# Interleaving each LayerNorm with the residual loop in front of it, in a four-layer attention and gMLP kernel

## The chip, the cores and the metric

The kernel runs on one core of a Trainium2 chip. The metric is the device time of one execution in microseconds (us). The kernel before takes 2619.56 us, the median of 5 runs (2618.32 to 2621.13). In what follows ScalarE is shown as ACT, VectorE as DVE, TensorE's matmuls as PE and its weight loads as PEld.

## The reference

A stream `x` of 2048 rows by 512 columns passes through four layers. Layers 1 and 3 are multi-query attention (A), layers 2 and 4 are gMLP (B). Each has a LayerNorm in front and a residual add behind. Both A layers share their weights, and so do both B layers.

```python
x = A_x
x = x + _A_ref(_layernorm(x), wq, wk, wv, wo)        # 32 heads of 16, one k and one v
x = x + _B_ref(_layernorm(x), w_in, w_sp, b_sp, w_out)
x = x + _A_ref(_layernorm(x), wq, wk, wv, wo)
x = x + _B_ref(_layernorm(x), w_in, w_sp, b_sp, w_out)
```

`_layernorm` subtracts the row mean and divides by `sqrt(var + 1e-5)`. It has no weights of its own.

## The kernel before

X stays in SBUF as 16 tiles of 128 rows by 512 columns, so every LayerNorm works on 16 tiles. A small scheduler takes instructions in program order: each engine has its own in-order list, and waits between engines are semaphores. **The order in which the Python code adds instructions is therefore the order in which each engine runs them.** No compiler moves them later.

The residual loop of a layer makes a tile's output on TensorE, adds it to X on VectorE, and then takes the next LayerNorm's statistics of that tile, also on VectorE:

```python
def ln_stats_tile(tt, waits):                  # VectorE
    # bn_stats (X tile -> 6 numbers a row), bn_aggr (-> mean, var), then
    # lnve = var + LN_EPS
    ...

def emit_woproj(tt, bank):                     # residual loop of attention
    # 8 matmuls of 128x512 into one PSUM bank
    ...
    er = sch.add("dve", lambda v, tt=tt, bank=bank: v.tensor_tensor(
        X[:, tt, :], PS[:, bank, 0:D], X[:, tt, :], op=ALU.add), [last])
    ...
    if not is_last_layer:
        next_stats[tt] = ln_stats_tile(tt, [er])
...
for tt in range(NT):
    emit_woproj(tt, tt % 6)                    # gMLP's loop is alike, with 7 matmuls
```

When all 16 tiles are through, the next layer begins with a LayerNorm phase of its own. The phase normalises each tile on ScalarE, transposes it on TensorE with four matmuls against an identity matrix, and copies the transposed tile out of PSUM. The copies alternate between VectorE and ScalarE:

```python
def layernorm_phase(ev_stats):
    for tt in range(NT):
        ... # ScalarE: Sqrt.  VectorE: reciprocal, and nmr = -mean * reciprocal
    ...
    def finish_copy(item):
        ...
        if tt % 2 == 0:
            e_cp = sch.add("dve", lambda v, src=src, dst=dst: v.tensor_copy(dst, src), [last_pe])
        else:
            e_cp = sch.add("act", lambda s, src=src, dst=dst: s.activation(dst, src, ACT.Copy), [last_pe])
        ...
    for tt in range(NT):
        bufi = tt % 2                          # two xn buffers
        e_xn = sch.add("act", ... xn2[:, bufi, :], X[:, tt, :], ACT.Identity,
                       bias=nmr, scale=reciprocal ...)
        bank = tt % 8
        for kc in range(KC):                   # KC = 4 transposes
            last_pe = sch.add("pe", ... PS[:, bank, ...], xn2[:, bufi, ...], ident ...)
        pend.append((tt, bank, last_pe))
        if len(pend) > 1:
            finish_copy(pend.pop(0))
    ...
```

The softmax here doesn't subtract the row's maximum and nothing guards it: scores larger than these inputs give would overflow.

## Time and profile before

The program is a row of stages that follow one another. I read their borders from the trace: the first kT matmul, the load of the Exp table, the first residual add, the first matmul of the gMLP layer, and so on. A few matmul records can be missing from a trace, so such a border may be off by a few tenths of a us. "Boundary" is the stretch from the first residual add of one layer to the first matmul of the next.

| stage of before | us | how often |
|---|---|---|
| start: loads, statistics, first LayerNorm | 37.3 | 1 |
| q, k, v projections | 24.9, 25.3 | 2 |
| attention core (Exp stage) | 936.5, 936.8 | 2 |
| boundary attention to gMLP | 44.1 | 2 |
| GELU of w_in | 93.6 | 2 |
| rest of gMLP up to its first residual add | 156.1 | 2 |
| boundary gMLP to attention | 44.1 | 1 |
| last residual loop and output | 26.7 | 1 |

The page's chain of waits, followed back from the last instruction, gives shares of the span by engine and then by line:

```profile
ACT 68%; PE 19%; DVE 11%; issue 1%; DMA 0%; SPq 0%; ACTq 0%
ACT regA L473 62%; PE PS L689 8%; PE PS L488 4%; PE PS L457 3%; DVE regB L599 2%; ACT g_sg L597 2%; PE PS L391 2%; DVE lnst L313 2%; ACT g_zb L580 1%; ACT xn L346 1%; PE PS L708 1%; DVE zst L626 1%; DVE regB L659 1%; DVE X L524 1%; DVE regA L497 1%
```

The Exp on ScalarE (line 473 of before) holds 62% of the span in this chain. It lies outside the change (ScalarE is busy 922.68 of 936.48 us in row 2 below), so the question is what the four stretches with a LayerNorm cost. Line numbers are those of the kernel that the lines come from. The table of stretches (columns: stretch in us, its length, busy us and instruction count of each engine, granted TensorE clock, DMA share, GB/s) shows the start, one Exp stage, and the two parts of one attention-to-gMLP boundary:

```profile
core 0: us, PE busy (x) PEld busy (x) DVE busy (x) ACT busy (x) POOL busy (x), PEclk, DMA share, GB/s
4.84:37.33 32.49, 9.52 (x64) 5.57 (x65) 24.03 (x88) 18.75 (x39) 5.29 (x6) 1.00 0.62 162
62.21:998.69 936.48, 803.04 (x4138) 154.41 (x4138) 148.53 (x97) 922.68 (x690) 0.00 (x0) 0.67 0.02 5
998.69:1026.50 27.81, 17.49 (x80) 7.01 (x80) 26.15 (x66) 3.04 (x15) 0.00 (x0) 0.89 0.99 197
1026.50:1042.81 16.31, 9.52 (x64) 5.56 (x65) 8.96 (x40) 15.71 (x24) 0.00 (x0) 0.50 0.96 180
```

Rows 3 and 4 are the point. In the residual part VectorE is busy 26.15 of 27.81 us while ScalarE works 3.04. In the LayerNorm part it is the other way round: ScalarE 15.71 of 16.31, VectorE 8.96. So the two halves of a boundary have different limiting engines and follow one another. The timeline of before shows one tile of the residual part (columns: start, duration, engine, line, operation, operands, count, and in brackets the idle time before and who ended it):

```profile
1000.42 0.68 DVE L524 TENSOR_TENSOR X<-PS,X 128x512 bf16<-128x512 f32 x1
...
1001.14 0.69 DVE L313 BATCH_NORM_STATS2 lnst<-X 128x6 f32<-128x512 bf16 x1
...
1001.87 0.18 DVE L315 BATCH_NORM_AGGREGATE lnmv<-lnst 128x2 f32<-128x6 f32 x1
1002.08 0.15 DVE L316 TENSOR_SCALAR lnve<-lnmv 128x1 f32<-128x1 f32 x1
1002.15 0.68 DVE L524 TENSOR_TENSOR X<-PS,X 128x512 bf16<-128x512 f32 x1
1002.27 0.20 ACT L323 ACTIVATE lnve<-lnve 128x1 f32<-128x1 f32 x1 [1.53 <-DVE lnve L316]
```

From add to add is 1002.15 - 1000.42 = 1.73 us, all of it VectorE. ScalarE waits 1.53 us of each period for its one square root. The timeline of the LayerNorm part of before:

```profile
1033.06 0.60 ACT L340 ACTIVATE xnT<-PS 128x512 bf16<-128x512 f32 x1
...
1033.56 1.50 ACT L346 ACTIVATE xn<-X,lnr 128x512 bf16<-128x512 bf16 x2
1033.76 0.69 DVE L338 CAST xnT<-PS 128x512 bf16<-128x512 f32 x1 [1.22 <-PE PS L353]
...
1034.41 1.10 PE L353 MATMUL PS<-ident,xn 128*128 128x128 bf16 x6 [0.69 <-ACT xn L346]
1035.06 0.60 ACT L340 ACTIVATE xnT<-PS 128x512 bf16<-128x512 f32 x1
```

Two tiles take 2.00 us on ScalarE (1033.06 to 1035.06: one copy and two normalisations, back to back), so a tile costs 1.00 us, and PE and VectorE both wait for ScalarE. Two groups of instructions of before, the copies on ScalarE and its square roots, will be compared with those of after (columns: line, engine, operation, operands, count, then busy us, mean ns of one, and idle us of the engine just before them):

```profile
L340 ACT ACTIVATE xnT<-PS 128x512 bf16<-128x512 f32 x32 | 19.0, 594 | 2.8 <-PE PS L353 2.8
L323 ACT ACTIVATE lnve<-lnve 128x1 f32<-128x1 f32 x64 | 13.0, 203 | 202.1 <-DVE lnve L316 202.1
```

ScalarE stood idle for 202.1 us in front of its 64 square roots. Of these, 117.3 us are the three waits for the first tile of a boundary (13.78, 89.78 and 13.77 us), which end before the residual loop is under way; 68.9 us are the 45 waits of 1.53 us inside the three residual loops; the rest is in the start.

### The profile page before, as it was taken

How to read it: one execution, taken by the hardware profiler on the slowest of the kernel's cores; microseconds unless marked ns; L12 is line 12 of the kernel's file. 1: busy time of each engine (PE TensorE's matmuls, PEld its weight loads, DVE VectorE, ACT ScalarE, POOL GpSimd, SP SyncE). 2: the span in 40 equal slices, each digit the busy share in tenths (PEclk: the TensorE clock that was granted, in tenths of full speed). 3: DMA queues.
4: the chain of work that ended last, by engine and by line, in shares of the span. 5: the costliest groups of instructions: out<-in, count | busy, mean ns of one | idle time of the engine just before them, and what ended most of it. 6: DMA issues, size and time to landing. Idle time of an engine off the chain costs nothing.

```text
span 2619.3 us, 25140 instructions
## 1 busy us (share of the span) xinstructions
PE 2153.3 (82%) x10680; PEld 526.5 (20%) x10680; DVE 716.5 (27%) x1246; ACT 2084.6 (80%) x1814; POOL 128.8 (5%) x139
## 2 busy tenths in 40 slices
PE   5888888888888887659978888888888888875599
PEld 2111111111111113113431111111111111131143
DVE  5011111112111116673341111111211111177732
ACT  4999999999999993442059999999999999933410
POOL 1000000000000000331000000000000000003300
PEclk9666766667666667679976676666766666676799
DMA  3000000000000006000000000000000000060000
GB/s 93 5 5 5 5 5 5 5 8 5 5 5 5 5 5 133 1 0 1 1 1 5 5 5 5 5 5 9 5 5 5 5 5 5 8 130 1 0 1 33
DMA packets 85488, 34.93 MB, mean 13 GB/s; under 512 B 75680, under 2 KB 80800, under 8 KB 85376
## 3 DMA queue, kind: packets, MB, share of 16 engines
q1 hardware_dynamic: 84832, 30.58, 5.5%
q0 software_dynamic: 544, 2.76, 0.3%
q8 instruction: 83, 1.36, 0.2%
q14 instruction: 29, 0.24, 0.0%
HBM read 6.05 MB, written 2.10 MB: 3 GB/s over the span
## 4 chain that ended last, share of the span: by engine, by line
ACT 68%; PE 19%; DVE 11%; issue 1%; DMA 0%; SPq 0%; ACTq 0%
ACT regA L473 62%; PE PS L689 8%; PE PS L488 4%; PE PS L457 3%; DVE regB L599 2%; ACT g_sg L597 2%; PE PS L391 2%; DVE lnst L313 2%; ACT g_zb L580 1%; ACT xn L346 1%; PE PS L708 1%; DVE zst L626 1%; DVE regB L659 1%; DVE X L524 1%; DVE regA L497 1%
## 5 line engine op out<-in xcount | busy, mean ns | idle before, releaser
L473 ACT ACTIVATE regA<-PS 128x1536 bf16<-128x1536 f32 (+1 forms) x1376 | 1840.4, 1611 | 3.8
L488 PE MATMUL PS<-regA 128*32 128x512 bf16 x4096 | 989.8, 534 | 7.8 <-DVE regA L497 7.1
L457 PE MATMUL PS<-regA 32*128 32x512 bf16 x4096 | 732.8, 526 | 260.3 <-ACT regA L473 243.3
L497 DVE COPY regA<-PS 128x512 f32<-128x512 f32 x64 | 41.2, 686 | 1459.9 <-PE PS L488 1459.9
L457 PEld LDWEIGHTS PS<-regA 32*128 32x128 bf16 x4096 | 140.5, 96 | 1025.5 <-ACT regA L473 1002.8
L488 PEld LDWEIGHTS PS<-regA 128*32 128x32 bf16 x4096 | 158.4, 100 | 525.1 <-issue 487.0
L510 DVE RECIPROCAL regA<-regA 128x512 f32<-128x512 f32 x64 | 214.3, 3349 | 115.7 <-DMA regA<-regA 115.7
L583 POOL TENSOR_TENSOR g_t<-g_zb 128x512 bf16<-128x512 bf16 x120 | 118.5, 990 | 2275.4 <-ACT g_zb L580 2275.1
L689 PE MATMUL PS<-regA,regB 128*128 128x512 bf16 x896 | 203.1, 380 | 1.7 <-ACT g_zb L580 1.7
L323 ACT ACTIVATE lnve<-lnve 128x1 f32<-128x1 f32 x64 | 13.0, 203 | 202.1 <-DVE lnve L316 202.1
L671 PE MATMUL PS<-xnT,w_in 128*128 128x512 bf16 x224 | 80.7, 505 | 73.0 <-ACT g_zb L580 72.9
L580 ACT ACTIVATE g_zb<-PS 128x512 bf16<-128x512 f32 x120 | 67.5, 568 | 91.3 <-DVE regB L599 80.9
L597 ACT ACTIVATE g_sg<-g_t 128x512 bf16<-128x512 bf16 x120 | 72.1, 601 | 81.4 <-DVE g_t L595 81.0
L639 PE MATMUL PS<-w_in,xnT 128*128 128x512 bf16 (+1 forms) x256 | 78.8, 464 | 44.8 <-ACT g_zb L580 44.5
L689 PEld LDWEIGHTS PS<-regA,regB 128*128 128x128 bf16 x896 | 83.1, 98 | 107.5 <-issue 14.5
L599 DVE TENSOR_TENSOR regB<-g_zb,g_sg 128x512 bf16<-128x512 bf16 x120 | 77.8, 649 | 85.8 <-ACT g_sg L597 85.8
L353 PE MATMUL PS<-ident,xn 128*128 128x128 bf16 x256 | 38.9, 307 | 72.6 <-ACT xn L346 48.4
L695 DVE TENSOR_TENSOR regB<-PS,regB 128x512 bf16<-128x512 f32 x56 | 37.8, 689 | 138.3 <-PE PS L692 138.3
L521 PE MATMUL PS<-wop,regB 128*128 128x512 bf16 x256 | 59.9, 398 | 1.8 <-DVE X L524 1.8
L595 DVE TENSOR_TENSOR g_t<-g_t,g_zb 128x512 bf16<-128x512 bf16 x120 | 49.9, 416 | 4.1
L346 ACT ACTIVATE xn<-X,lnr 128x512 bf16<-128x512 bf16 x64 | 48.7, 804 | 0.5
L708 PE MATMUL PS<-w_out,regB 128*128 128x512 bf16 x224 | 48.7, 379 | 0.0
(56 smaller groups left out, 599.7 us busy)
## 6 DMA issues: line engine op xcount, KB each, us to landing
regA<-regA SPq DMA_DIRECT2D x256, 32.0 KB, 1.9
X<-in_A_x_dram SPq DMA_DIRECT2D x4, 512.0 KB, 5.5
out_dram<-X SPq DMA_DIRECT2D x4, 512.0 KB, 2.9
w_in<-in_B_w_in_dram POOLq DMA_DIRECT2D x1, 1792.0 KB, 9.4
w_out<-in_B_w_out_dram POOLq DMA_DIRECT2D x1, 896.0 KB, 11.5
wq<-in_A_wq_dram SPq DMA_DIRECT2D x1, 512.0 KB, 8.2
wop<-in_A_wo_dram SPq DMA_DIRECT2D x4, 128.0 KB, 4.4
regA<-in_B_w_sp_dram SPq DMA_TRANSPOSE x32, 5.1
```

The costliest lines, as they stand in the source:

```text
L346: e_xn = sch.add("act", lambda s, tt=tt, bufi=bufi: s.activation(xn2[:, bufi, :], X[:, tt, :], ACT.Identity, bias=lnr[:, 1, tt:tt + 1], sc ...
L457: last = sch.add("pe", lambda tt_, g=g, e=e, bank=bank, t=t, b=b, cq=cq: tt_.matmul(PS[:, bank, 0:QW], kT[32 * g:32 * g + 32, e, t * 128:( ...
L473: ev_act[u] = sch.add("act", lambda s, q=q, slot=slot, n=n: s.activation(Ering[:, slot, 0:n * QW], PS[:, 3 * q:3 * q + n, :].rearrange("p ...
L488: last = sch.add("pe", lambda tt_, j=j, i=i, t=t, pp=pp, slot=slot: tt_.matmul(PS[32 * j:32 * j + 32, 6 + pp, 0:QW], vaug[:, t, :], Ering[ ...
L510: v2 = sch.add("dve", lambda v, pp=pp: v.reciprocal(rden[pp], denb[pp]), [pt])
L580: a1 = sch.add("act", lambda s, bi=bi, w=w, zap=zap: s.activation(g_zb[:, bi, 0:w], zap, ACT.Copy), [pe_last] + gbuf_free[bi])
L583: p1 = sch.add("pool", lambda g, bi=bi, w=w: g.tensor_tensor(g_t[:, bi, 0:w], g_zb[:, bi, 0:w], g_zb[:, bi, 0:w], op=ALU.mult), [a1])
L597: a2 = sch.add("act", lambda s, bi=bi, w=w: s.activation(g_sg[:, bi, 0:w], g_t[:, bi, 0:w], ACT.Sigmoid, scale=GELU_SIG_SCALE), [v3])
L599: v4 = sch.add("dve", lambda v, bi=bi, w=w, dst_ap=dst_ap: v.tensor_tensor(dst_ap, g_zb[:, bi, 0:w], g_sg[:, bi, 0:w], op=ALU.mult), [a2])
L639: last = sch.add("pe", lambda t, tt=tt, kc=kc, f0=f0, w=w, bank=bank: t.matmul(PS[:, bank, 0:w], xnT[:, kc, tt * 128:(tt + 1) * 128], w_in ...
L671: last = sch.add("pe", lambda t, fc=fc, kc=kc, t0=t0, tw=tw, bank=bank: t.matmul(PS[:, bank, 0:tw], w_in[:, kc, fc * 128:(fc + 1) * 128], ...
L689: last = sch.add("pe", lambda t, fc=fc, sc=sc, t0=t0, tw=tw, bank=bank: t.matmul(PS[:, bank, 0:tw], z2n[:, sc, fc * 128:(fc + 1) * 128], w ...
```

## The change

The intent is to run the LayerNorm of a tile as soon as that tile's residual add is done, inside the residual loop, rather than in a phase behind it. The start does the same directly behind its statistics.

```diff
-        def layernorm_phase(ev_stats):
-            ... (all 16 square roots, then 16 tiles of normalise, transpose, copy)
+        class LNPipe:
+            def tile(self, tt, stats_ev, x_ready):
+                e_sq = ... ACT.Sqrt ...
+                self.pend_sc.append((tt, e_sq, x_ready))
+                if len(self.pend_sc) > 1:             # scaling lags one tile
+                    self._scale(*self.pend_sc.pop(0))
+            def _scale(self, tt, e_sq, x_ready):
+                ... reciprocal and nmr on VectorE, normalise on ScalarE into xn2[tt % 6]
+                self.pend_pe.append((tt, bufi, e_xn))
+                if len(self.pend_pe) > 3:             # transposes lag four tiles
+                    self._trans(*self.pend_pe.pop(0))
+            def _trans(self, tt, bufi, e_xn):
+                bank = 5 + tt % 3                     # three PSUM banks
+                ... four transposes
+                self.pend.append((tt, bank, last_pe, holder))
+                if len(self.pend) > 1:                # copies lag five tiles
+                    self._finish(self.pend.pop(0))
+            def _finish(self, item):
-                if tt % 2 == 0:
+                if False:
                     ... copy on VectorE
                 else:
                     ... copy on ScalarE
+            def flush(self): ... empties the three queues
 
-                if not is_last_layer:
-                    next_stats[tt] = ln_stats_tile(tt, [er])
+                if next_ln is not None:
+                    st = ln_stats_tile(tt, [er])
+                    next_ln.tile(tt, st, er)
 
-                emit_woproj(tt, tt % 6)
+                emit_woproj(tt, tt % 5)
+            if next_ln is not None:
+                next_ln.flush()
```

Three smaller things come with it. There are six xn buffers (they lie on the end of a region that is free at that time) in place of two. The residual matmuls use banks 0 to 4, so that 5 to 7 are left for the transposes. All 64 PSUM copies run on ScalarE, where 32 ran on VectorE before.

More of the change, by code (lines that the diff above doesn't have):

```diff
@@ L62, in _flatten_waits @@
             wl.extend(_flatten_waits(w))
+        elif isinstance(w, dict):
+            assert "ev" in w, "unresolved pipeline placeholder"
+            wl.extend(_flatten_waits([w["ev"]]))
         else:
@@ L228, in build @@
         zve = sb("zve", [128, NT], FP32)
-        xn2 = sb("xn2", [128, 2, D], BF16)
         xnT = sb("xnT", [128, KC, S], BF16)
@@ L240, in build @@
         regB = sb("regB", [128, regB_elems], BF16)
+        xn2 = regB[:, regB_elems - 6 * D:regB_elems].rearrange("p (b d) -> p b d", b=6)
         z1T = regB[:, 0:NFC * S].rearrange("p (a b) -> p a b", a=NFC)
@@ L318, in ln_stats_tile, with __init__ @@
             return e3
-        def layernorm_phase(ev_stats):
-            e_nmr_t = {}
-            for tt in range(NT):
-                e_sq = sch.add("act", lambda s, tt=tt: s.activation(
-                    lnve[:, tt:tt + 1], lnve[:, tt:tt + 1], ACT.Sqrt), [ev_stats[tt]])
+        class LNPipe:
+            def __init__(self):
+                self.ev_xnT = {}
+                self.pend = []
+                self.xn_free = [None] * 6
+                self.pend_pe = []
+                self.pend_sc = []
+            def tile(self, tt, stats_ev, x_ready):
+                e_sq = sch.add("act", lambda s, tt=tt: s.activation(
+                    lnve[:, tt:tt + 1], lnve[:, tt:tt + 1], ACT.Sqrt), [stats_ev])
+                self.pend_sc.append((tt, e_sq, x_ready))
+                if len(self.pend_sc) > 1:
+                    self._scale(*self.pend_sc.pop(0))
+            def _scale(self, tt, e_sq, x_ready):
                 e_r = sch.add("dve", lambda v, tt=tt: v.reciprocal(lnr[:, 0, tt:tt + 1], lnve[:, tt:tt + 1]), [e_sq])
-                e_nmr_t[tt] = sch.add("dve", lambda v, tt=tt: v.scalar_tensor_tensor(
+                e_nmr = sch.add("dve", lambda v, tt=tt: v.scalar_tensor_tensor(
                     out=lnr[:, 1, tt:tt + 1], in0=lnmv[:, tt, 0:1], scalar=-1.0, in1=lnr[:, 0, tt:tt + 1],
                     op0=ALU.mult, op1=ALU.mult), [e_r])
-            ev_xnT = {}
-            xn_free = [None, None]
-            pend = []
-            def finish_copy(item):
-                tt, bank, last_pe = item
-                src = PS[:, bank, 0:KC * 128].rearrange("p (kc c) -> p kc c", kc=KC)
-                dst = xnT[:, :, tt * 128:(tt + 1) * 128]
-                if tt % 2 == 0:
-                    e_cp = sch.add("dve", lambda v, src=src, dst=dst: v.tensor_copy(dst, src), [last_pe])
-                else:
-                    e_cp = sch.add("act", lambda s, src=src, dst=dst: s.activation(dst, src, ACT.Copy), [last_pe])
-                bank_free[bank] = [e_cp]
-                ev_xnT[tt] = e_cp
-            for tt in range(NT):
-                bufi = tt % 2
+                bufi = tt % 6
                 e_xn = sch.add("act", lambda s, tt=tt, bufi=bufi: s.activation(
@@ L348, in layernorm_phase @@
                     bias=lnr[:, 1, tt:tt + 1], scale=lnr[:, 0, tt:tt + 1]),
-                    [e_nmr_t[tt], xn_free[bufi], X_tile_ready[tt]])
-                bank = tt % 8
+                    [e_nmr, self.xn_free[bufi], x_ready])
+                self.pend_pe.append((tt, bufi, e_xn))
[3 more added lines that the diff above has]
+                bank = 5 + tt % 3
                 last_pe = None
@@ L356, in layernorm_phase, with flush, events @@
                         ([e_xn, ev_ident] + bank_free[bank]) if kc == 0 else [])
-                bank_free[bank] = ["pending"]
-                xn_free[bufi] = last_pe
-                pend.append((tt, bank, last_pe))
-                if len(pend) > 1:
-                    finish_copy(pend.pop(0))
-            while pend:
-                finish_copy(pend.pop(0))
-            return [ev_xnT[tt] for tt in range(NT)]
+                holder = {}
+                bank_free[bank] = [holder]
+                self.xn_free[bufi] = last_pe
+                self.pend.append((tt, bank, last_pe, holder))
+                if len(self.pend) > 1:
+                    self._finish(self.pend.pop(0))
+            def _finish(self, item):
+                tt, bank, last_pe, holder = item
+                src = PS[:, bank, 0:KC * 128].rearrange("p (kc c) -> p kc c", kc=KC)
+                dst = xnT[:, :, tt * 128:(tt + 1) * 128]
+                if False:
+                    e_cp = sch.add("dve", lambda v, src=src, dst=dst: v.tensor_copy(dst, src), [last_pe])
+                else:
+                    e_cp = sch.add("act", lambda s, src=src, dst=dst: s.activation(dst, src, ACT.Copy), [last_pe])
+                holder["ev"] = e_cp
+                bank_free[bank] = [e_cp]
+                self.ev_xnT[tt] = e_cp
+            def flush(self):
+                while self.pend_sc:
+                    self._scale(*self.pend_sc.pop(0))
+                while self.pend_pe:
+                    self._trans(*self.pend_pe.pop(0))
+                while self.pend:
+                    self._finish(self.pend.pop(0))
+            def events(self):
+                assert len(self.ev_xnT) == NT, "LN pipeline incomplete"
+                return [self.ev_xnT[tt] for tt in range(NT)]
         evac_ctr = [0]
@@ L373, in evac_copy, with attention_layer @@
             return sch.add("dve", lambda v, src=src, dst=dst: v.tensor_copy(dst, src), waits)
-        def attention_layer(ev_stats, is_last_layer):
-            all_xnT = layernorm_phase(ev_stats)
+        def attention_layer(all_xnT, next_ln):
             ev_kT = []
@@ L563, in attention_layer, with gmlp_layer @@
             for tt in range(NT):
-                emit_woproj(tt, tt % 6)
-        def gmlp_layer(g_wsp, ev_stats, is_last_layer):
+                emit_woproj(tt, tt % 5)
+            if next_ln is not None:
+                next_ln.flush()
+        def gmlp_layer(g_wsp, all_xnT, next_ln):
             for sc in range(NKT):
@@ L569, in gmlp_layer @@
                         waits=list(shared_state["regA_free"]))
-            all_xnT = layernorm_phase(ev_stats)
             gbuf_free = [[] for _ in range(GNB)]
@@ L702, in gmlp_layer @@
             for tt in range(NT):
-                bank = gi % 8
+                bank = tt % 5
                 tci = (tt * 128) // 512
@@ L714, in gmlp_layer @@
                 X_tile_ready[tt] = er
-                if not is_last_layer:
-                    next_stats[tt] = ln_stats_tile(tt, [er])
+                if next_ln is not None:
+                    st = ln_stats_tile(tt, [er])
+                    next_ln.tile(tt, st, er)
                 gi += 1
-        next_stats = [ln_stats_tile(tt, [x_part_group[tt]]) for tt in range(NT)]
+            if next_ln is not None:
+                next_ln.flush()
         X_tile_ready = [x_part_group[tt] for tt in range(NT)]
+        shared_state = {"regA_free": []}
+        ln0 = LNPipe()
+        for tt in range(NT):
+            st = ln_stats_tile(tt, [x_part_group[tt]])
+            ln0.tile(tt, st, x_part_group[tt])
+        ln0.flush()
+        cur_ln = ln0
         bi_ = 0
-        shared_state = {"regA_free": []}
         for li, Lt in enumerate(layer_types):
-            cur_stats = list(next_stats)
             is_last = (li == len(layer_types) - 1)
-            if cfg.get("barrier", False):
-                sch.barrier()
+            next_ln = None if is_last else LNPipe()
+            all_xnT = cur_ln.events()
             if Lt == "A":
-                attention_layer(cur_stats, is_last)
+                attention_layer(all_xnT, next_ln)
             else:
-                gmlp_layer(g_wsp_list[bi_], cur_stats, is_last)
+                gmlp_layer(g_wsp_list[bi_], all_xnT, next_ln)
                 bi_ += 1
+            cur_ln = next_ln
         nparts = 4 if NT % 4 == 0 else 1
```

## The prediction

> **What bounds it now.** The chain of waits is 62% the Exp on ScalarE in the two attention stages (from the stretches view: 62 to 986 us and 1361.5 to 2286 us, ScalarE busy 922 of 924 us in each). The change doesn't touch them. The u product (109 us twice, TensorE busy 108.7) and the GELU stages (about 139 us twice, a ScalarE/VectorE/Pool loop) aren't touched either. What it touches are the four LayerNorm stretches. In the timeline of before:
> - Start: statistics from 4.8 us at 1.0 us a tile, then 16 square roots done, then normalise/transpose/copy from 21.3 to 37.3 us. This phase is ScalarE-bound: two xn (0.75 us apart) and one copy (0.5 us) make 2.0 us per two tiles; ScalarE is busy 15.7 of 16.5 us.
> - Attention to gMLP (twice): VectorE runs residual add 0.72, statistics 0.73, aggregate and epsilon 0.29, 1.73 us a tile, from 998.7 to 1026.4 us; only then the LayerNorm phase, 16.3 us, to 1042.8. ScalarE is busy 3 of the first 27.8 us.
> - gMLP to attention: the same from 1292.5 to 1320.3, then 16.3 us, to 1336.7.
>
> **What the change does.** The LayerNorm of a tile follows its residual add in a pipeline, transposes 4 tiles behind on TensorE, so most of the 16.3 us phase hides under the residual phase. All 16 PSUM copies move to ScalarE (VectorE loses 32 casts of 0.69 us). No work is removed. I considered table switches, since Sqrt now alternates with Identity and Copy. The Trainium skill ("ScalarE: Activation LUTs", Table sets) says that copy and identity are in every set; before's trace agrees (one load of 1.28 us at the first Sqrt, none between Sqrt and xn and copy), and the built program still has 12 loads. So no cost.
>
> **Costs of the merged phase, per tile.** VectorE: 1.73 plus reciprocal and nmr 0.27 = 2.0 us. TensorE: after attention 8 matmuls at 0.216 = 1.73 plus four transposes about 0.33 = 2.06; after gMLP 7 at 0.216 = 1.51 plus 0.33 = 1.84. ScalarE: sqrt 0.15-0.2, xn 0.75, copy 0.5 = about 1.45. So after attention VectorE and TensorE are nearly tied, about 2.06 us; after gMLP VectorE, 2.0; at the start (no residual add; VectorE 1.28) ScalarE, about 1.45.
>
> The merged phase thus lengthens by 0.27-0.33 us x 16 = 4.3-5.2 us, and a tail stays after the last residual add: statistics, sqrt, xn, then five ScalarE copies, two of which gate the last transposes: about 5.7 us from the last add to the last transpose (before: 18.1).
>
> Gains, all on the critical path (estimates from the above): start, last transpose at about 30.6 instead of 37.3: 6.7; attention to gMLP 7.5 each, twice; gMLP to attention 8.4. Sum 30 us. TensorE may also be warmer at the next stage (before: granted clock 0.50 in the LayerNorm phase, first 8 matmuls 0.43 us each): 0 to 2 us a boundary, mostly lost since the tail is sparse too.
>
> **Prediction: 2589 us**, 1.2% less; 80% range 2578 to 2600. Faster by over 2%: 0.03; within 2%: 0.95; slower: 0.02.
>
> **Right if:** first kT matmuls start near 30.6 us; the residual phases take about 32-33 us rather than 27.8; the LayerNorm-only part falls from 16.3 to about 4-5 us; Exp stages keep 924 us.
>
> **Wrong if:** the merged loop settles above 2.2 us a tile (waits between the four engines, or a half clock on TensorE after its wait for the first transpose), which costs 3 us per boundary for each 0.2; ScalarE at the start takes more than 1.6 us a tile; or GELU stages shift their rhythm by a few us.

## The result, and the profile after

The kernel after takes 2583.82 us, the median of 7 runs (2581.33 to 2584.86). Before takes 2619.45 us in 13 runs (2618.32 to 2621.13). The ratio is 0.9864 (95% interval 0.9854 to 0.9874), which is within 2%. A ratio here is the mean time of one kernel's fast runs over that of the other's of the same rounds, so it is not quite the ratio of the quoted medians. The result is correct.

The gain of the medians is 35.6 us. The prediction had 30.

| stage | before | after | gain |
|---|---|---|---|
| start, to first kT matmul | 37.33 | 28.54 | 8.79 |
| boundary attention to gMLP, 1st | 44.12 | 35.27 | 8.85 |
| boundary gMLP to attention | 44.14 | 35.28 | 8.86 |
| boundary attention to gMLP, 2nd | 44.13 | 35.27 | 8.86 |
| **these four together** | | | **35.4** |
| Exp stages, both | 1873.25 | 1873.85 | -0.6 |
| projections and GELU, two of each | 237.4 | 231.9 | 5.6 |
| rest of gMLP before the residual add, both | 312.2 | 312.7 | -0.5 |

The four places give 35.4 us, which is the gain of the medians within the spread. The spans of the two profiled executions differ by more, 2619.3 - 2579.5 = 39.8 us. This pair is an extreme one: the profiled run of before was its slowest (2621.13), that of after its fastest (2581.33). The excess sits in the projections and the GELU stages. I come back to it below, because "TensorE is warmer there" would be a tempting reading.

The same views of after. The chain of waits by engine:

```profile
ACT 69%; PE 18%; DVE 11%; issue 1%; DMA 0%; SPq 0%; ACTq 0%
ACT regA L497 64%; PE PS L715 8%; PE PS L512 4%; PE PS L481 3%; DVE regB L625 3%; ACT g_sg L623 2%; PE PS L415 2%; ACT g_zb L606 1%; DVE lnst L316 1%; PE PS L734 1%; DVE zst L652 1%; DVE regB L685 1%; DVE X L548 1%; DVE regA L521 1%; PE PS L718 1%
```

The shares barely changed (Exp is now line 497), and the chain alone would not have told where 36 us came from. The table of stretches does (the first boundary is cut where the last VectorE instruction of the loop is done):

```profile
core 0: us, PE busy (x) PEld busy (x) DVE busy (x) ACT busy (x) POOL busy (x), PEclk, DMA share, GB/s
4.84:28.54 23.70, 9.40 (x65) 5.57 (x65) 18.88 (x80) 20.66 (x47) 5.29 (x6) 1.00 0.84 222
52.47:989.06 936.59, 799.49 (x4130) 153.40 (x4130) 148.52 (x96) 922.80 (x690) 0.00 (x0) 0.67 0.02 5
989.06:1021.70 32.64, 25.27 (x140) 12.07 (x140) 29.96 (x97) 20.24 (x42) 0.00 (x0) 0.84 1.02 194
1021.70:1024.33 2.63, 1.28 (x12) 0.98 (x13) 0.00 (x0) 2.63 (x7) 0.00 (x0) 0.83 1.08 178
```

The residual part grew from 27.81 to 32.64 us and now holds 20.24 us of ScalarE work that used to stand behind it. What is left of the LayerNorm part is 2.63 us, from 16.31. The timeline of after, one tile of the merged loop:

```profile
1004.78 0.68 DVE L548 TENSOR_TENSOR X<-PS,X 128x512 bf16<-128x512 f32 x1
1004.90 0.81 ACT L344 ACTIVATE regB<-X,lnr 128x512 bf16<-128x512 bf16 x1
1005.50 0.70 DVE L316 BATCH_NORM_STATS2 lnst<-X 128x6 f32<-128x512 bf16 x1
1005.62 0.58 ACT L374 ACTIVATE xnT<-PS 128x512 bf16<-128x512 f32 x1
1006.23 0.18 DVE L318 BATCH_NORM_AGGREGATE lnmv<-lnst 128x2 f32<-128x6 f32 x1
...
1006.35 0.39 PE L356 MATMUL PS<-ident,regB 128*128 128x128 bf16 x4
1006.45 0.15 DVE L319 TENSOR_SCALAR lnve<-lnmv 128x1 f32<-128x1 f32 x1
...
1006.52 0.15 DVE L339 RECIPROCAL lnr<-lnve 128x1 f32<-128x1 f32 x1
...
1006.64 0.20 ACT L332 ACTIVATE lnve<-lnve 128x1 f32<-128x1 f32 x1 [0.44 <-DVE lnve L319]
1006.71 0.16 DVE L340 SCALAR_TENSOR_TENSOR lnr<-lnmv,lnr 128x1 f32<-128x1 f32 x1
```

VectorE again has no gap that ends in a wait: add 0.72, statistics 0.73, aggregate 0.22, epsilon 0.07, reciprocal 0.19, nmr 0.07 (start to start, and to the next add), 2.00 us a tile. From first to last, the 16 adds go from 989.06 to 1018.79, which is 1.98 us for each of 15 intervals: the first is 1.73, because a tile's reciprocal and nmr come one tile late, and the other 14 are 2.00. ScalarE idles only 0.44 us in the tile shown. The timeline of the tail, from the last residual add:

```profile
1018.79 0.68 DVE L548 TENSOR_TENSOR X<-PS,X 128x512 bf16<-128x512 f32 x1
...
1020.25 0.40 PE L356 MATMUL PS<-ident,regB 128*128 128x128 bf16 x4 [1.60 <-ACT xnT L374]
...
1022.25 0.40 PE L356 MATMUL PS<-ident,regB 128*128 128x128 bf16 x4 [1.60 <-ACT xnT L374]
1022.80 2.04 ACT L374 ACTIVATE xnT<-PS 128x512 bf16<-128x512 f32 x4
...
1024.33 0.63 PE L665 MATMUL PS<-w_in,xnT 128*128 128x512 bf16 x1
```

Twice the transposes wait 1.60 us for a copy (line 374): the ring of three PSUM banks is full, and its copies stand in ScalarE's queue behind normalisations. The groups of after:

```profile
L374 ACT ACTIVATE xnT<-PS 128x512 bf16<-128x512 f32 x64 | 35.7, 590 | 0.0
L332 ACT ACTIVATE lnve<-lnve 128x1 f32<-128x1 f32 x64 | 13.0, 203 | 153.7 <-DVE lnve L319 153.7
```

ScalarE took over all copies (19.0 to 35.7 us), and its idle time in front of the square roots fell from 202.1 to 153.7 us: from 68.9 to 28.8 us inside the residual loops, and from 16.0 to 5.6 in the start.

### The profile page after: what moved, and what is told of

It reads as the page before. It is cut to its first block, busy times and chain, and to the rows that moved or that the text cites. A ratio compares the mean times of both kernels' runs of the same rounds, so it can differ in the third digit from the quotient of the medians.

```text
span 2579.5 us, 25082 instructions
## 1 busy us (share of the span) xinstructions
PE 2147.6 (83%) x10680; PEld 522.3 (20%) x10680; DVE 697.3 (27%) x1214; ACT 2100.4 (81%) x1846; POOL 128.9 (5%) x139
## 4 chain that ended last, share of the span: by engine, by line
ACT 69%; PE 18%; DVE 11%; issue 1%; DMA 0%; SPq 0%; ACTq 0%
ACT regA L497 64%; PE PS L715 8%; PE PS L512 4%; PE PS L481 3%; DVE regB L625 3%; ACT g_sg L623 2%; PE PS L415 2%; ACT g_zb L606 1%; DVE lnst L316 1%; PE PS L734 1%; DVE zst L652 1%; DVE regB L685 1%; DVE X L548 1%; DVE regA L521 1%; PE PS L718 1%
## 5 line engine op out<-in xcount | busy, mean ns | idle before, releaser
L332 ACT ACTIVATE lnve<-lnve 128x1 f32<-128x1 f32 x64 | 13.0, 203 | 153.7 <-DVE lnve L319 153.7
L356 PE MATMUL PS<-ident,regB 128*128 128x128 bf16 x256 | 30.4, 256 | 49.3 <-ACT regB L344 24.9
L545 PE MATMUL PS<-wop,regB 128*128 128x512 bf16 x256 | 66.8, 414 | 0.0
L344 ACT ACTIVATE regB<-X,lnr 128x512 bf16<-128x512 bf16 x64 | 52.1, 813 | 3.2
```

## The experiments

**The theory (T1, overlap):** a boundary becomes shorter because most of the phase behind the last residual add vanishes, while each tile of the residual loop gets about 0.27 us longer on VectorE, which sets the pace of the merged loop.

**The rivals:** (R1) the shift of the copies to ScalarE makes the gain; (R2) more buffers make it; (R3) TensorE stays warm through the boundary, and the next stages start faster; (R4) the start makes most of it. Further, VectorE, TensorE and ScalarE were predicted close together in the merged loop, so which of them sets the pace had to be tested.

The runs of one kernel lie within 1 to 3.5 us, and twice within 5 to 5.5 us (ph_warm, and before in its group); kernels of one group below ran on one chip with their own runs of before (medians 2618.2, 2619.1 and 2619.36).

### Half of the change: only the start (start_only)

The start uses the pipeline; the three boundaries keep the separate phase, as code of the new class's form.

```diff
-        next_stats = [ln_stats_tile(tt, [x_part_group[tt]]) for tt in range(NT)]
+        ln0 = LNPipe()                      # interleaved, as in after
+        ...
+            next_ln = None if is_last else LNPhased()   # statistics first, all else at flush()
```

(The diff is against before; the residual matmuls use the banks of before.)

> The changed kernel with the pipelined LayerNorm only at the start of the program; at the three layer boundaries the LayerNorm is a phase of its own again, as in the kernel before. If the gain is four separate hidden phases that add up, this keeps the start's share alone: the first key projection moves from 37.3 to 28.5 us as in the changed kernel's trace, plus about 1 us for a warmer TensorE, so about 2610 us (9 to 10 us less than before). Rival, that the gain is made at one place (for instance in the GELU stages, or by a shifted rhythm of the Exp stage): far from that, 2618 or 2590 us.

Measured: 2609.94 us (2609.22 to 2610.89), before 2618.2, ratio 0.997 (0.9956 to 0.9983). The first kT matmul starts at 28.95 us and the three boundaries take 44.5, about as in before (44.1). So the start is worth about 8.3 us, and R4 falls: it is one place of four.

### The other half: only the three boundaries (bounds_only)

```diff
-        ln0 = LNPipe()
+        ln0 = LNPhased()
...
-            next_ln = None if is_last else LNPhased()
+            next_ln = None if is_last else LNPipe()
```

(The diff is against start_only; the banks of the residual matmuls are those of after.)

> The counterpart of the start-only kernel: the LayerNorm in a phase of its own at the start, pipelined at the three boundaries. If the gains are separate and add up, it gets the rest: the whole change gained 36 to 37 us and the start alone 8 to 9, so 27 to 28 us less than before, about 2591 us, with boundaries of 35.3 us.

Measured: 2592.84 us (2591.76 to 2593.08), before 2619.36, ratio 0.9899 (0.9884 to 0.9914). That is 26.5 us for three boundaries. With the start's 8.3 us the halves sum to 34.8, against 35.6 for the whole. Within the spread, the gains add up, and each place gives nearly the same.

### The copies alone, in the phase (ph_actcopy)

```diff
-                if tt % 2 == 0:
+                if False:
                     e_cp = sch.add("dve", ... v.tensor_copy ...)
```

> The kernel before with one part of the change alone: all PSUM copies of the transposed tiles on ScalarE. If moving the copies were itself a gain (VectorE relieved of 32 casts), this is faster than before. My theory says the reverse: the separate phase is bound by ScalarE, 1.0 us a tile with half the copies, 0.75 + 0.5 = 1.25 us with all of them, so each of four phases grows from 16.3 to about 20 us: 4 x 4 = 16 us slower, about 2635 us.

Measured: 2629.07 us (2627.77 to 2630.36), ratio 1.0044 (1.0031 to 1.0056), 10.9 us slower. R1 falls: in the old structure this part of the change is a loss, since ScalarE limits the phase. The size was expected larger. The trace shows a tile period of 1.18 us where I had 1.25: the normalisation takes 0.70 us start to start before a copy, and the copy 0.48.

### The buffers alone, in the phase (ph_buf6)

```diff
-        xn2 = sb("xn2", [128, 2, D], BF16)
+        xn2 = regB[:, regB_elems - 6 * D:regB_elems].rearrange("p (b d) -> p b d", b=6)
...
-                bufi = tt % 2
+                bufi = tt % 6
```

> The kernel before with another part of the change alone: six buffers for the normalised tiles, at the end of the region that the z2 tensor uses, instead of two of their own. If a shortage of buffers had held the separate phase up, this is faster. My theory says it is not: ScalarE is busy 15.7 of the phase's 16.5 us and loses 0.5 us in 64 tiles ahead of the normalise, so 2618 us and boundaries of 44.1 us, unchanged within 1 us.

Measured: 2618.51 us (2617.54 to 2619.57), ratio 0.9998 (0.9985 to 1.001). R2 falls.

### The merged loop with alternating copies (pipe_altcopy)

This undoes one part of the change in after.

```diff
-                if False:
+                if tt % 2 == 0:
                     e_cp = sch.add("dve", ... v.tensor_copy ...)
```

> The changed kernel with the copies alternating between VectorE and ScalarE again, as before. Theory: the merged loop is bound by VectorE at 2.0 us a tile, so a 0.7 us cast on every second tile adds 0.36 us a tile, 5.7 us per boundary, less about 1 us for a shorter tail; with the start (1.27 us a tile, VectorE) four times about 4.7, so about 2584 + 19 = 2603 us, with a period of about 2.36 us a tile in the three boundary loops. Rival, that the loop is bound by TensorE (1.95 us a tile after attention) or by a chain of waits through all engines: within 5 us of the changed kernel, or slower by much more than 19.

Measured: 2593.11 us (2592.86 to 2593.91), ratio 0.9907 (0.9893 to 0.992), 9.3 us slower than after's 2583.82 (of other rounds). So interleaving without the switch of the copies gains 25.1 us (2618.2 to 2593.11), and the same switch that costs 10.9 us in the phase earns about 9 us in the merged loop: the limiting engine there is another one. From the sixth add on, the adds stand 2.0 and 2.6 us apart in turn, so a cast costs the loop 0.60 us, not the 0.7 that I had put in. The boundaries are only 2.6 us longer (37.85 us), where I had expected 4.7. I had counted all eight casts of a boundary in the loop; but the copies lag five tiles, so only five of the eight stand between the first and the last add: 5 x 0.6 = 3.0 us (the loop takes 32.7 us, in after 29.7). The other three fall into the tail, which is 5.15 us, against 5.54 in after. Hence the factor of two.

### More VectorE work per tile (pipe_dve2)

The reciprocal and nmr are made a second time into a spare tile. Nothing else changes.

```diff
+                e_r = sch.add("dve", ... v.reciprocal(lnx[:, 0, tt:tt + 1], lnve[:, tt:tt + 1]), [e_sq])
+                e_dup = sch.add("dve", ... nmr again, into lnx[:, 1, tt:tt + 1] ..., [e_r])
```

> The changed kernel with the two small VectorE instructions of each tile's LayerNorm (reciprocal and the product with the mean, 0.27 us together) done twice, the second time into a scratch tensor that nobody reads. If VectorE bounds the merged loops, every place gets 16 x 0.27 = 4.3 us longer: the three boundaries 35.3 to about 39.6 us, the start 28.5 to about 32.8, in all 17 us, about 2601 us. If TensorE (1.95 us a tile after attention) or ScalarE (1.28 us a tile at the start) or the handshakes between them bound the loop and VectorE has slack, the cost is less: near 0 where the slack exceeds 0.27 us a tile.

Measured: 2597.5 us (2596.38 to 2597.93), ratio 0.9918 (0.9904 to 0.9931), 15.3 us slower than after on the same chip (2582.19). The timeline of pipe_dve2, one tile after attention:

```profile
1004.39 0.68 DVE L553 TENSOR_TENSOR X<-PS,X 128x512 bf16<-128x512 f32 x1
...
1006.39 0.16 DVE L344 RECIPROCAL lnx<-lnve 128x1 f32<-128x1 f32 x1
...
1006.58 0.16 DVE L345 SCALAR_TENSOR_TENSOR lnx<-lnmv,lnx 128x1 f32<-128x1 f32 x1
1006.66 0.68 DVE L553 TENSOR_TENSOR X<-PS,X 128x512 bf16<-128x512 f32 x1
```

The period is 1006.66 - 1004.39 = 2.27 us, the old 2.00 and the 0.27 of the added pair. The boundaries grew from about 35.3 to 39.0 (39.3 after gMLP), the start from 28.9 to 32.7. I had expected 17 us for 16 pairs at each place; only 14 of the 15 intervals between the adds hold a pair, and 14 x 0.27 = 3.8 us is what each place lost (3.7 to 3.8; after gMLP 3.2 against after_again, whose own boundary there was 0.8 us long). So VectorE sets the pace of all three merged loops, and at the start it has no slack to speak of either.

### Less VectorE work per tile (pipe_eps)

The add of epsilon moves from VectorE into the bias operand of the square root on ScalarE.

```diff
-            e3 = sch.add("dve", lambda v, tt=tt: v.tensor_scalar(
-                lnve[:, tt:tt + 1], lnmv[:, tt, 1:2], LN_EPS, None, op0=ALU.add), [e2])
-            return e3
+            return e2
...
-                    lnve[:, tt:tt + 1], lnve[:, tt:tt + 1], ACT.Sqrt), [stats_ev])
+                    lnve[:, tt:tt + 1], lnmv[:, tt, 1:2], ACT.Sqrt, bias=epst[:, 0:1]), [stats_ev, ev_eps])
```

> The changed kernel with epsilon in the bias operand of the square root, so that VectorE loses one small instruction a tile (and the wait of the square root moves to the aggregate). In the trace of the combined version the VectorE period went from 2.0 to 1.79 us a tile after gMLP and to TensorE's 1.95 us after attention. If the limits are VectorE after gMLP, TensorE close behind it after attention, and ScalarE at the start (its square root gets a pointer operand more), then the gMLP-to-attention boundary shortens by 15 x 0.21 = 3.1 us, to about 32.2, the two attention-to-gMLP ones by 15 x 0.05 = 0.7, to about 34.5 us, and the start hardly: about 2578 us. If VectorE is the only limit, all four shorten by 3 us: about 2571 us.

Measured: 2574.47 us (2574.22 to 2575.07), ratio 0.983 (0.9817 to 0.9844), 9.4 us faster than after (of other rounds). The timeline of pipe_eps, TensorE during one tile after attention (at 1004 us) and then two residual adds after gMLP (at 1287 us):

```profile
1003.98 0.39 PE L356 MATMUL PS<-ident,regB 128*128 128x128 bf16 x4
...
1004.42 1.67 PE L545 MATMUL PS<-wop,regB 128*128 128x512 bf16 x7
...
1005.93 0.39 PE L356 MATMUL PS<-ident,regB 128*128 128x128 bf16 x4
...
1287.12 0.68 DVE L737 TENSOR_TENSOR X<-PS,X 128x512 bf16<-128x512 f32 x1
...
1288.91 0.68 DVE L737 TENSOR_TENSOR X<-PS,X 128x512 bf16<-128x512 f32 x1
```

After gMLP the period falls to 1288.91 - 1287.12 = 1.79 us; the boundary takes 31.89 us, as expected (32.2). After attention the period is at first 1.76 to 1.79 us, while TensorE has a lead, and then stays at 1005.93 - 1003.98 = 1.95, where TensorE shows no wait: the transposes and eight matmuls fill it (one of the eight records is missing). Eight matmuls at 0.216 us are 1.73, which leaves 0.22 for the four transposes. So **the next limit after attention is TensorE at 1.95 us a tile**, only 0.05 below VectorE's 2.00. The boundary took 33.07 us, less than the 34.5 that I expected. At the start nothing moved (28.61 against 28.54). The edit also lengthens the square root there, from 0.20 to 0.29 us: ScalarE takes 1.37 us a tile (1.28 in after), and VectorE waits about 0.2 us a tile for it. So at the start ScalarE bounds the loop of pipe_eps; this run doesn't show which of the two is first in after.

### TensorE kept busy in the phase (ph_warm)

Before, with two matmuls added per tile of the LayerNorm phase. Their results are overwritten by the transposes that follow.

```diff
+                for d in range(2):
+                    sch.add("pe", lambda t, bank=bank, tt=tt: t.matmul(
+                        PS[:, bank, 0:D], ident[:, :], X[:, tt, :], start=True, stop=True), ...)
                 last_pe = None
                 for kc in range(KC):
```

> The kernel before with two dummy 128x512 matmuls (identity by the X tile, into the PSUM bank that the tile's transposes then overwrite) ahead of each tile's transposes, so that TensorE does not idle in the LayerNorm phases. The result stays right. In the trace of the changed kernel about 5.9 us of the gain lie after the LayerNorm, in the first groups of matmuls of the next stage. If those come from TensorE being warmer, this kernel gains 4 to 7 us over the one before (2613 to 2616 us) although nothing is overlapped, with first matmuls of the next stage at 0.22 instead of 0.43 us. If warmth does not matter, or the LayerNorm phases are slowed by the extra matmuls: 2619 us or more.

Measured: 2615.33 us (2610.64 to 2616.09), ratio 0.9988 (0.9975 to 1.0), 2.9 us less than before's 2618.2, just at the edge of what these runs resolve, and between the two outcomes that I had written down (4 to 7 us, or none). The stretch of its LayerNorm phase:

```profile
core 0: us, PE busy (x) PEld busy (x) DVE busy (x) ACT busy (x) POOL busy (x), PEclk, DMA share, GB/s
1024.60:1041.28 16.68, 13.62 (x93) 7.18 (x96) 8.93 (x39) 15.36 (x24) 0.00 (x0) 0.80 0.85 167
```

The granted clock rose from 0.50 (row 4 of the table of before) to 0.80 and the phase kept its length, since ScalarE bounds it. The projections fell to 23.1 us each and the GELU stages to 91.0, but the rest of gMLP rose from 156.1 to 157.7 both times, for a reason that no run shows. GELU and the rest together take 497.4 us, as in ph_actcopy (497.4), which adds no matmuls; before has 499.5. What sets ph_warm apart is the projections: both together 46.3 us, in every other kernel 47.9 to 50.2. Their first matmuls come 0.22 us apart, as expected (in before 0.43). So a warmer TensorE does shorten the next stage, by a few us in all. The three boundaries and the start became 0.5 us longer each, as they did in ph_buf6 (0.4) without any extra matmul. R3 can't be the main cause: with the clock raised to 0.80 in the phase, the total moved by 2.9 us.

### The tail (pipe_tail)

After, with the last three tiles' transposes in banks 1 to 3 (free by then), and the last copies issued after the last normalisations and alternating between VectorE and ScalarE.

```diff
-                bank = 5 + tt % 3
+                bank = 5 + tt % 3 if tt < NT - 3 else 1 + (tt - (NT - 3))
...
-                if len(self.pend) > 1:
+                if len(self.pend) > 1 and tt < NT - 5:
...
                 while self.pend:
-                    self._finish(self.pend.pop(0))
+                    self._finish(self.pend.pop(0), dve=(k % 2 == 0))
```

> The changed kernel with the last five tiles rearranged: the last normalise runs on ScalarE ahead of the remaining PSUM copies, half of these copies go to VectorE, which is idle by then, and the last three tiles transpose into PSUM banks that the residual tiles have freed. If the tail behind the last residual add (5.5 us in the changed kernel's trace) is made by the copies that stand in ScalarE's queue and gate the last transposes, it shortens by about 1.5 us at each of the four places: boundaries 35.3 to about 33.8 us, 5 to 6 us in all, about 2578 us. If the tail is the latency of the chain add, statistics, sqrt, normalise, transpose alone, nothing changes.

Measured: 2574.18 us (2573.41 to 2575.45), ratio 0.983 (0.9817 to 0.9844), 8.0 us less than after on the same chip. The timeline of its tail (the last residual add is at 1016.74):

```profile
1020.43 0.40 PE L356 MATMUL PS<-ident,regB 128*128 128x128 bf16 x4 [0.31 <-ACT regB L344]
1020.66 0.38 PE L667 MATMUL PS<-w_in,xnT 128*128 128x512 bf16 x1
```

From the last add to the first gMLP matmul is now 1020.66 - 1016.74 = 3.9 us, against 5.5 in after, and the last transposes wait for the normalisation (line 344) rather than for a free bank. That shows that after's tail was set by the ring of three banks and its copies. The three boundaries took 33.64, 34.87 and 33.65 us and the start 27.48: 5.9 us less than in after_again, as expected (5 to 6). The other 2 us of the 8.0 lie outside these places and are no larger than the spread. The three edits were not tried one by one.

### All of it together (pipe_best)

Pipe_eps and pipe_tail together, and the first residual tile of attention started before the last normalisation of the attention output, so that its add stands earlier in VectorE's list.

```diff
+                        if u_last == NU - 1:
+                            ...
+                            emit_woproj(0, 0)
                         for pp in range(2):
-                            emit_evac_rest(cq, b, pp, v1s[pp])
+                            emit_evac_norm(cq, b, pp, pts[pp])
...
-            for tt in range(NT):
+            for tt in range(1, NT):
                 emit_woproj(tt, tt % 5)
```

> The previous version and two more changes at the places that the trace names: epsilon goes into the square root's bias operand, which takes 0.07 us a tile off VectorE (1 us a boundary, if VectorE bounds the loop; TensorE at 1.95 us a tile is the next limit after attention), and the first tile's output projection, residual add and statistics run on VectorE while it waits for the last denominator transfers of attention (3.2 us idle in the trace; TensorE delivers the tile some 3 us after the last Exp, so about 1.3 us is won, twice). About 5 us less than the previous version, about 2573 us.

Measured: 2563.41 us (2562.64 to 2564.51), ratio 0.9789 (0.9775 to 0.9802), correct. It beats both kernels: 55.7 us less than before and 18.8 less than after on the same chip. I had expected about 2573. The main difference is that the removed epsilon add is worth 0.21 us a tile and not 0.07, the mis-sizing that pipe_eps then measured by itself. Exp stage and first boundary together take 966.6 us, in pipe_tail 969.6. Of these 3.0 us about 2.2 are pipe_eps's part (its first boundary took 33.07 us, after's 35.27). That leaves about 1 us for the early first tile, which is no more than the Exp stages differ between executions (935.7 to 937.4 us): its gain is not shown.

### After once more, on the chip of the three variants (after_again)

The kernel of after without an edit.

> The changed kernel itself, once more, as the reference for the three that follow on the same chip: 2581 to 2585 us, with 35.3 us from the first residual add of a boundary to the first matmul of the next layer, three times.

Measured: 2582.19 us (2581.58 to 2583.44), before 2619.1, ratio 0.9861 (0.9847 to 0.9874). The result repeats. One boundary differed in its trace: gMLP to attention took 36.11 us, not 35.28. TensorE had waited 2.00 us for a copy in the middle of that loop, and the 7 matmuls behind it took 2.48 us rather than about 1.7. In after TensorE has the same wait (1.99 us, up to 1286.25), but the matmuls behind it take 1.67 us. What differs is the granted clock: 1.00 from 1286 to 1291 us in after, 0.66 in after_again. The same 36.11 shows in bounds_only (clock 0.66 behind the wait), and pipe_tail's 34.87 goes with the same drop (0.66 again). The prediction had named such a risk under "Wrong if", a half clock on TensorE after a wait; here it lasts for one or two tiles and costs 0.8 to 1.1 us at one place. Why the clock fell after this wait in some executions and not in others was not tried.

## Why the prediction was right, and where it was off

**Right:** the time (2583.8 inside 2578 to 2600), and the mechanism. Point by point:

- *"VectorE: 1.73 plus reciprocal and nmr 0.27 = 2.0 us"*: measured 2.00 in the timeline and 1.98 on average. That it sets the pace was shown by adding work (pipe_dve2: period 2.27) and by removing some (pipe_eps: 1.79 after gMLP). After attention the prediction had TensorE just ahead of it (2.06); the runs have VectorE ahead (2.00 against 1.95).
- *The residual phases take 32 to 33 us*: 32.6. *The LayerNorm-only part falls to about 4 to 5 us*: 2.6 in the first boundary, so better than said.
- *The tail, "about 5.7 us from the last add to the last transpose"*: 5.5 us from the last add to the first gMLP matmul, and for the stated reason, copies gating the last transposes (pipe_tail).
- *The Exp stages keep their time*: 936.5 and 936.6. *No cost of table switches*: both kernels' traces have 12 table loads of 1.28 us, though Sqrt now alternates with Identity and Copy. This agrees with the Trainium skill ("ScalarE: Activation LUTs", Table sets), which says that copy and identity are part of every set.
- *The interleaving itself*: the Trainium skill ("Perfetto Trace Analysis", Optimization Strategy) says that a kernel whose limiting engine changes over time may gain "by interleaving those regimes". The two rows of before with VectorE 26.15 of 27.81 us and ScalarE 15.71 of 16.31 us are such regimes, and interleaving them is worth 8.8 us at each place.

**Off, in size:** the sum of the gains was 30 us and came to 35.6. All terms erred on the same side, so no errors cancelled in the total. The terms:

| place | predicted gain | measured | the term that was mis-sized |
|---|---|---|---|
| start | 6.7 | 8.8 | ScalarE, about 1.45 us a tile predicted; measured 1.28 |
| attention to gMLP, each | 7.5 | 8.85 | the loop's growth, 5.2 predicted (with TensorE at 2.06 us a tile); measured 3.7 (VectorE at 2.00; TensorE at most 1.95) |
| gMLP to attention | 8.4 | 8.86 | the loop's growth, 4.3 predicted; measured 3.7 |
| warmer TensorE in the next stages | 0 | about 0 to 3 | see below |

At the start I had added up a square root of 0.15 to 0.2 us, the normalisation and the copy. In the timeline of after the square root starts 0.09 us before the normalisation that follows it (17.36 and 17.45), so it costs the loop about half of what I had put in. Start to start the three take 1.28 us, and VectorE takes 1.27: they are tied. That fits pipe_dve2, where more VectorE work slowed the start, and pipe_eps, where less did not speed it up.

At the boundaries the sum has two terms, loop and tail. From first to last residual add, the gMLP-to-attention boundary takes 26.0 us in before (1292.55 to 1318.56) and 29.7 in after (1273.05 to 1302.79): 3.7 us more. From the last add to the first matmul of the next layer it takes 18.1 us in before and 5.5 in after: 12.6 us less. The difference is 8.9. The tail was predicted well (18.1 to 5.7, so 12.4). The loop's growth was predicted too large: I multiplied 0.27 to 0.33 us by 16 tiles, but 16 tiles have 15 intervals, and the first of them holds no reciprocal and nmr yet. 14 x 0.27 is 3.8 us. (The recorded gains, 7.5 and 8.4, are also 0.3 more than 12.4 less 5.2 and 12.4 less 4.3; the record doesn't say why.)

After attention I took four transposes as 0.33 us. In before's LayerNorm phase, at a granted clock of 0.50, the transposes of a tile start 0.08 to 0.11 us apart. In the merged loop of pipe_eps they start 0.056 us apart (granted clock 1.00 from 1004 to 1016 us), so four take 0.22 us, which makes TensorE's period 1.95 us. So a duration that is read at a low clock must not be carried into a stage with a full one. (The record doesn't show from which lines I had read the 0.33.)

**Warm TensorE.** I wrote "0 to 2 us a boundary, mostly lost". The two profiled executions show 5.6 us less in the projections and GELU stages, and one is tempted to credit the clock. But the spread of these stages between executions is as large: two of each took 237.4 us in before, but 234.2 in ph_buf6 and 232.9 in ph_actcopy, which both keep the separate phase. In after they took 231.9, in after_again 232.4, in pipe_altcopy 234.1. The mean of those three kernels with the phase is 234.8, of the three without 232.8: about 2 us in all, a difference within the spread. TensorE is warmer there in after, in part: in the first 5 us of the first GELU stage the granted clock is 0.50 in before, 0.75 in after and 1.00 in ph_warm, whose same stages took 228.3 us in sum, less than in any other kernel here. But ph_warm got only 2.9 us net. So the term is at most a few us, and "mostly lost" stands as far as these runs can tell.

**What stays open:** why the rest of gMLP took 1.6 us longer in ph_warm, why the clock falls in some executions behind TensorE's wait in the gMLP-to-attention boundary (0.8 us), and how much the early first residual tile in pipe_best gives by itself. The lags of the pipeline and the split of the PSUM banks were not varied, other than in the tail.

## What to carry to other kernels

When two neighbouring stages have different limiting engines, cost the merged loop engine by engine from durations in the trace, and take the largest sum: the gain is the removed phase, less what the loop's limiting engine gains in work, less the tail that is left behind the last tile. Which engine should get the movable work (here the PSUM copies) depends on the structure: the same switch lost 10.9 us in the separate phase and earned about 9 us in the merged loop, so decide it after the merge. And compare several executions of a stage before crediting it with a few us from one pair of profiles.

## What the Trainium skill lacked or had wrong

- "VectorE: DVE Perf Modes", The DRAIN you can't avoid, says that a semaphore between VectorE operations "costs nothing extra here". For the smallest operations the start-to-start time does depend on whether the next one needs the result: 0.19 to 0.22 us when it does (aggregate to the epsilon add, 1006.23 to 1006.45; reciprocal to nmr, 1006.52 to 1006.71), 0.07 when it doesn't (epsilon add to reciprocal of the tile before). In pipe_eps, where the next operation after the aggregate no longer needs its result, it starts 0.10 us later (1288.57 to 1288.67) and not 0.22. Dropping a 0.15 us operation therefore saved 0.21 us a tile (2.00 to 1.79) and not its 0.07. The page is not contradicted in its own case, eight copies that take 13.88 us together, so far larger operations; what it lacks is a figure for small ones.
- "ScalarE: Activation LUTs", What ACT_TABLE_LOAD costs, gives 1283 ns and about 1380 ns of drain for each switch. The trace agrees on the load (12 loads of 1.28 us in both kernels), but shows no such drain: at the start of the first Exp stage of before, a copy ends at 62.19 us, the load runs from 62.21, and the Exp starts at 63.50, so 1.31 us from the end of the copy to the start of the Exp.
- "TensorE: Matmul & The Clock Gate", Part 1, says that the default is throttled and activity releases it, and for how long TensorE must be busy, but not how dense the activity has to be. In before's LayerNorm phase TensorE was shown busy 9.52 of 16.31 us by small identity matmuls and was granted 0.50; with two more matmuls of 128x512 per tile it was shown busy 13.62 of 16.68 us and was granted 0.80. That is a mean: its transposes start 0.106 us apart up to 1031 us and 0.056 from 1031.6 on, 6 us after the first.
